# The second MLP of an RWKV and two-MLP kernel: Strassen's method for its input product, tokens as the moving operand of its output product

## The chip, the cores and the metric

The kernel is one program on one core of a Trainium2 chip. The metric is the device time of one execution in microseconds (us). The engines that matter are TensorE (PE in the rows; PEld is its weight load), VectorE (DVE), ScalarE (ACT), GpSimd (POOL) and SyncE (SP, which only starts DMA transfers here). Each engine works through its own queue of instructions in order, and they wait for one another by semaphores.

## The reference, cut to what matters

```python
# attention: batch 4, 8 heads, 768 steps, head size 48
for t in range(S):
    cur = np.einsum('bhd,bhe->bhde', u[None] * kt, vt)
    y[:, :, t] = np.einsum('bhd,bhde->bhe', rt, state + cur)
    state = wt[:, :, :, None] * state + np.einsum('bhd,bhe->bhde', kt, vt)
x = y as (3072 tokens, 384)
# first MLP: 384 -> 1536 (gated) -> 384
x = (x @ w_a) * (x @ w_b) @ w_out
# second MLP: 384 -> 2048 -> 384
h = x @ w_in
g = np.maximum(h, 0.0) + alpha * np.minimum(h, 0.0)
return g @ w_out
```

All inputs and the output are float32. The kernel gets close to float32 products by splitting every operand into a high and a low part (`hi`, `lo`) and adding three products: high by high, low weight by high, high weight by low. Each `128x128` by `128x512` product is therefore three matmuls.

## The kernel before, in words

The attention and the first MLP run interleaved and are not touched in what they compute. The first MLP ends by writing its result, tile by tile, to a scratch tensor in DRAM (`x2d`).

The second MLP (`mlp2`, L1098) then takes the 3072 tokens in six chunks `c` of 512 (128 steps of each of the four sequences) and the 2048 features in 16 groups `f` of 128. For each chunk, `load_x2` (L1067) reads 384 x 512 values back and splits them. For each group, `gh` makes `h` = three contraction tiles by three part products = nine matmuls with 512 token columns moving, into a PSUM bank (`hp`, `hb`). DVE applies the leaky function (`neg`, `pos`: L1145, L1149), ACT makes the high part of `g` (L1154) and DVE the low part (L414, the helper `tt`). The output product `out2` has `g` as the stationary operand (128 features x 128 tokens) and the weights as the moving one: 384 columns, four token tiles, three part products, twelve matmuls for each `f` and `c`, into four accumulators (`acd0` to `acd2` and `hb2`). Four groups' input products and four groups' output products alternate (`RUN = 4`), so PSUM holds four `h` banks and four accumulators. A finished chunk is copied out by ACT and DVE (L1191, L1189) and stored by SP with rows of 1536 bytes (L1194).

The weights are loaded once (`load_w`, L427, DMAs from the POOL queue at L443) and turned into high and low parts by ACT (L453, L464) and DVE (L459, L468). All 32 tiles of the second MLP stay in SBUF for all chunks.

The order of all instructions is made before the build by a planner (`Tasks`). Each piece of work is added with its engine, an estimated duration, a priority, what it reads and writes, and the buffer that it takes; a list scheduler runs forward in time, keeps what is urgent by a backward pass, repeats this eight times and issues the best order. All stages pass through it together, so a change in the second MLP also shifts the order of earlier work.

Of the kernel before, what the change touches and what calls it, by code (L numbers as in the profile page):

```python
# [367 lines left out]
def rwkv_then_moe_kernel(  # L368
# [698 lines left out]
    def load_x2(c, p):  # L1067
        st = {}
        xn = f"xx{c}"
        for kt in range(3):  # L1070
            s = f"x2r{c}_{kt}"

            def ld(kt=kt):
                st[kt] = P2["p"].tile([128, 512], F32, tag="x2r", name="x2r", bufs=3)
                for i in range(2):
                    nc.sync.dma_start(out=st[kt][:, 256 * i:256 * i + 256], in_=x2d[2 * c + i, :, kt])

            def hi(kt=kt):
                if kt == 0:
                    X["2", c] = xp.tile([128, 2, 3, 512], F32R, tag="x", name="x", bufs=2)  # L1080
                nc.scalar.copy(X["2", c][:, 0, kt], st[kt])

            def lo(kt=kt):
                tt(X["2", c][:, 1, kt], st[kt], X["2", c][:, 0, kt].bitcast(F32), ALU.subtract)

            add("SP", 1.2, p - 20, ld, r=[f"x2d{2 * c}_{kt}", f"x2d{2 * c + 1}_{kt}", "p2"], w=[s], alloc=("x2r", s), nbytes=128 * 2048, packet=1024)
            add("ACT", act(512), p, hi, r=[s], w=[f"{xn}/{kt}h"], alloc=("x", xn) if kt == 0 else None)
            add("DVE", dve(512), p, lo, r=[s, f"{xn}/{kt}h"], w=[f"{xn}/{kt}l"])
        return [f"{xn}/{kt}{z}" for kt in range(3) for z in "hl"]
# [294 lines left out]
```

## Time and profile before

| | us |
|---|---|
| runs (three) | 991.46, 991.49, 995.54 |
| median | 991.49 |
| the profiled execution: its own time | 992.03 |
| its span, first to last instruction | 990.3 |
| PE busy | 973.9 (98%) |
| DVE busy | 713.6 (72%) |
| ACT busy | 366.8 (37%) |
| POOL busy | 60.6 (6%) |

The profile shows one execution; its own time is 0.5 us above the median of the runs, and 1.7 us longer than its span. Busy shares are means over stages that differ much, so the stage of the second MLP has to be cut out by time. Matmuls overlap, so the duration in a row (390 ns for one of 512 columns) is longer than the distance from one to the next.

### The profile page before, as it was taken

What the parts mean: (1) busy time and instruction counts of PE and PEld (TensorE: products, weight loads), DVE (VectorE), ACT (ScalarE), POOL (GpSimd) and SP (SyncE); (2) the same over time, 40 slices, a digit from 0 to 9 for tenths busy, and PEclk for the clock granted to TensorE, in tenths of its full rate; (3) what the DMA queues carried; (4) which work ended last, traced back from release to release, by engine and by line L of the source; (5) the groups of instructions that cost most, each with busy time, mean ns of one, the idle gap of its engine ahead of it and who ended that gap; (6) DMA issues with size and microseconds to landing.
All of it is one profiled execution on the core that took longest, in us unless ns stands there. A gap on an engine that the chain in (4) does not pass through costs nothing.

```text
span 990.3 us, 20850 instructions
## 1 busy us (share of the span) xinstructions
PE 973.9 (98%) x8802; PEld 821.1 (83%) x8802; DVE 713.6 (72%) x1215; ACT 366.8 (37%) x783; POOL 60.6 (6%) x113
## 2 busy tenths in 40 slices
PE   7999999999999999999999999999999999999998
PEld 3668777888888887887888888999999999999998
DVE  8989999797989999989735784555463645554543
ACT  0667572625444445452536662211111212111111
POOL 1111111000100100010003211000000000000000
PEclk9999999999999999999999999999999999999999
DMA  8897963404243342433026640020100100000000
GB/s 217 192 260 215 258 155 97 131 18 131 54 127 88 109 115 61 112 102 103 15 75 198 195 152 33 1 64 1 32 33 1 32 32 1 32 1 1 33 1 32
DMA packets 84559, 86.97 MB, mean 88 GB/s; under 512 B 62001, under 2 KB 71345, under 8 KB 83185
## 3 DMA queue, kind: packets, MB, share of 16 engines
q1 hardware_dynamic: 77296, 54.18, 21.1%
q0 software_dynamic: 7168, 31.45, 10.2%
q8 instruction: 69, 1.13, 0.5%
q14 instruction: 26, 0.20, 0.1%
HBM read 73.22 MB, written 11.01 MB: 85 GB/s over the span
## 4 chain that ended last, share of the span: by engine, by line
PE 78%; DVE 12%; issue 4%; DMA 3%; ACT 1%; POOL 1%; SPq 0%; DVEq 0%; POOLq 0%; ACTq 0%
PE acd L964 15%; PE hb L964 15%; PE pb L964 11%; PE acc L964 11%; PE pa L964 11%; PE hp L964 10%; DVE Tp L414 3%; DVE e L414 2%; DVE A L631 2%; PE psl L712 2%; PE psx L878 1%; DMA Tp<-in_rkw_t_dram 1%; DMA N<-in_rkw_n_dram 1%; DVE T L414 1%; DVE N L414 1%
## 5 line engine op out<-in xcount | busy, mean ns | idle before, releaser
L964 PE MATMUL acd<-w,g 128*128 128x384 f32 x864 | 192.6, 335 | 0.0
L1154 ACT CAST g<-g 128x512 fp32r<-128x512 f32 x96 | 59.7, 622 | 306.4 <-DVE g L1149 215.8
L964 PE MATMUL acc<-g,w 128*128 128x512 f32 x648 | 172.4, 396 | 0.0
L964 PE MATMUL pb<-x,w 128*128 128x512 f32 x648 | 160.5, 392 | 1.9 <-DVE a L414 1.9
L964 PE MATMUL pa<-x,w 128*128 128x512 f32 x648 | 162.1, 395 | 0.0
L964 PEld LDWEIGHTS acd<-w,g 128*128 128x128 f32 x864 | 154.2, 188 | 1.8
L1145 DVE TENSOR_SCALAR g<-hp,al 128x512 f32<-128x512 f32 x48 | 36.0, 751 | 156.2 <-PE hp L964 156.2
L964 PEld LDWEIGHTS pb<-x,w 128*128 128x128 f32 x648 | 121.0, 188 | 28.8 <-DVE a L414 3.4
L964 PEld LDWEIGHTS pa<-x,w 128*128 128x128 f32 x648 | 121.8, 189 | 26.9 <-issue 0.5
L964 PEld LDWEIGHTS acc<-g,w 128*128 128x128 f32 x648 | 118.8, 188 | 24.6
L414 DVE TENSOR_TENSOR Tp<-Tp 112x1024 f32<-112x1024 f32 (+2 forms) x132 | 106.6, 807 | 2.6 <-DMA Tp<-in_rkw_t_dram 2.1
L964 PE MATMUL hb<-x,w 128*128 128x512 f32 x432 | 102.9, 391 | 0.0
L964 PE MATMUL hp<-x,w 128*128 128x512 f32 x432 | 102.0, 389 | 0.0
L964 PEld LDWEIGHTS hp<-x,w 128*128 128x128 f32 x432 | 81.1, 188 | 16.8
L964 PEld LDWEIGHTS hb<-x,w 128*128 128x128 f32 x432 | 80.8, 188 | 16.0
L964 PE MATMUL hb<-w,g 128*128 128x384 f32 x288 | 92.5, 335 | 0.0
L1030 ACT CAST g<-a 128x512 fp32r<-128x512 f32 x72 | 44.6, 620 | 115.6 <-DVE a L414 90.9
L631 DVE TENSOR_REDUCE A<-e 128x16 f32<-128x768 f32 (+15 forms) x148 | 85.6, 578 | 0.9
L414 DVE TENSOR_TENSOR g<-g,g 128x512 fp32r<-128x512 f32 x96 | 64.1, 685 | 22.8 <-ACT g L1154 22.3
L414 DVE TENSOR_TENSOR a<-a,pb 128x512 f32<-128x512 f32 x72 | 49.1, 681 | 35.4 <-PE pb L964 35.2
L1021 ACT COPY a<-pa 128x512 f32<-128x512 f32 x72 | 41.9, 582 | 48.6 <-PE pa L964 40.4
L414 DVE TENSOR_TENSOR g<-a,g 128x512 fp32r<-128x512 f32 x72 | 49.4, 686 | 10.9 <-ACT g L1030 10.8
(80 smaller groups left out, 972.6 us busy)
## 6 DMA issues: line engine op xcount, KB each, us to landing
raw<-in_wt_dram POOLq DMA_DIRECT2D x68, 383.8 KB, 3.9
Tp<-in_rkw_t_dram SPq DMA_DIRECT2D x33, 448.0 KB, 6.6
N<-in_rkw_n_dram SPq DMA_DIRECT2D x10, 1152.0 KB, 5.5
x2d<-x POOLq DMA_DIRECT2D x36, 128.0 KB, 2.2
x2r<-x2d SPq DMA_DIRECT2D x36, 128.0 KB, 2.2
out_dram<-o SPq DMA_DIRECT2D x24, 192.0 KB, 1.9
V<-in_v_s_dram SPq DMA_DIRECT2D x11, 384.0 KB, 3.2
Z<-in_v_s_dram SPq DMA_DIRECT2D x44, 96.0 KB, 3.0
```

The costliest lines, as they stand in the source:

```text
L414: nc.vector.tensor_tensor(out=out, in0=a, in1=b, op=op)
L631: nc.vector.tensor_reduce(out=v[:, :, d:d + (n - 1) * (SUB + 1) + 1:SUB + 1], in_=part(st["e"], 0, n), axis=AX.X, op=ALU.add)
L712: nc.tensor.matmul(out=st["ps"][o0:o0 + ms, cc, q, zc * i:zc * i + zc], lhsT=t[b0:b0 + 48, 1, q0 + q, t0:t0 + ms], rhs=r[b0:b0 + 48, q0 + ...
L878: nc.tensor.matmul(out=st["ps"][32 * g:32 * g + 32, s // 4, 64 * cc:64 * cc + 64], lhsT=zt(cc, hd)[:, 4 * b + q, c0:c0 + 32], rhs=mt(hd)[: ...
L964: nc.tensor.matmul(out=out, lhsT=lhsT, rhs=rhs, start=start, stop=stop)
L1021: nc.scalar.copy(c["as", f, half][:, cs], c["a", f, half][:, cs])
L1030: nc.scalar.copy(c["g", f][:, 0, cs], c["as", f, half][:, cs])
L1145: nc.vector.tensor_scalar(out=st["m", f], in0=st["h", f], scalar1=0.0, scalar2=al[:, f:f + 1], op0=ALU.min, op1=ALU.mult)
L1154: nc.scalar.copy(st["g", f][:, 0], st["m", f])
```

## The change

The second MLP is rewritten. It works in cells: a pair of feature groups (`e` = 0 to 7, groups 2e and 2e+1) by a pair of blocks of 512 tokens. There are three passes `p` over the tokens (1024 tokens each) with eight cells in a pass.

- **Input product.** Two of the three contraction tiles are multiplied by Strassen's method in Winograd's form: seven block products in place of eight, with sums of token blocks (`t1` to `t4`, made by POOL in `load_x2`) and of weight blocks (`ws`, `wc`, made by POOL in `load_c`). The third contraction tile stays as four products. A cell has 11 block products of three matmuls, 33, in place of 36. The sums of the products are built in PSUM: bank X is accumulated in four steps, and after each of the first three ACT copies its state to SBUF (`snap`, L1223); bank Y has one such copy. The four results are then formed by DVE (`done`: a sum with a bank), followed by two ACT instructions (Relu) and one DVE instruction for the leaky function, and ACT and DVE for the high and low part of `g`.
- **Output product.** The weights are the stationary operand and `g` the moving one, with 512 tokens: nine matmuls for each group and block, into three accumulators for each of the two blocks (`oc00` to `oc12`). The results are transposed against the output's layout: DVE transposes blocks of 32 x 32 (`leave`, L1297) and the stores have runs of 128 bytes (L1304). In the last pass half of the stores are issued from the ACT queue.
- **Weights.** Five tiles for each `e` (`wi`, `ws`, `wc`, two `wp`), 40 in all. They do not stay in SBUF: pass 0 writes them to a DRAM scratch (`keeps`, L1178), passes 1 and 2 read them back on the SP queue (`again`, L1185).
- Some attention tiles (`M`, `Z`, `St`, `A16`) move to a pool that is freed after the attention.

```diff
+    def load_x2(p, pr):
...
+        split("b11", "xr00")
+        split("b22", "xr11")
+        comb("xr10", "xr11", "xr10", ALU.subtract)
+        split("t3", "xr10")
+        comb("xr00", "xr10", "xr00", ALU.add)
+        split("t2", "xr00")
...
+    def load_c(e, pr):
...
+        for i in range(4):
+            add(*SENG, pr, lambda i=i: sums(i), r=[r0, r1], w=[r1])
...
+    def keeps(e, pr):
+        for k, nm in CELL(e, 0):
+            add("SP", 0.6, pr, lambda k=k: nc.sync.dma_start(out=wsd[WI[k]], in_=W[k].bitcast(F32).rearrange("p z n -> p (z n)")),
+                r=[nm, nm + "/l"], w=[f"kept{nm}"], nbytes=128 * 3072)
+
+    def again(e, p, pr):
+        for (k, nm), (k0, nm0) in zip(CELL(e, p), CELL(e, 0)):
+            def ld(k=k, k0=k0):
+                W[k] = wp.tile([128, 2, 384], F32R, tag="w", name="w", bufs=NW)
+                nc.sync.dma_start(out=W[k].bitcast(F32).rearrange("p z n -> p (z n)"), in_=wsd[WI[k0]])
...
+            def snap(bank, o):
+                add("ACT", 0.58, pr - 20, lambda: nc.scalar.copy(SL[tm[o]], b[bank]), r=[f"h{bank}"], w=[tm[o]])
+
+            def done(bank, o, f, n):
+                x, q, g = tm[o], f"TQ{o % NQ}", f"G{par}{o}"
+                s = SL
+                add("DVE", 0.69, pr - 20, lambda: tt(s[x], s[x], b[bank], ALU.add), r=[f"h{bank}", x], w=[x])
+                if ACTP:
+                    add("ACT", 0.62, pr - 20, lambda: nc.scalar.activation(out=s[q], in_=s[x], func=ACTF.Relu, scale=-1.0), r=[x], w=[q])
+                    add("ACT", 0.62, pr - 20, lambda: nc.scalar.activation(out=s[x], in_=s[x], func=ACTF.Relu), r=[x], w=[x])
+                    add("DVE", 0.69, pr - 20, lambda: nc.vector.scalar_tensor_tensor(
+                        out=s[x], in0=s[q], scalar=al[:, f:f + 1], in1=s[x], op0=ALU.mult, op1=ALU.subtract), r=[x, q, "al"], w=[x])
...
+            pe(X, [(lambda: WA(0), "b11")], [nA], True, False)
+            snap(X, 0)
+            pe(Y, [(lambda: WB(0), "t1")], [nB], True, False)
+            snap(Y, 3)
+            pe(X, [(lambda: WB(1), "t2")], [nB], False, False)
+            snap(X, 1)
+            pe(Y, [(lambda: WC(0), "b22"), (lambda: WA(2), "b32")], [nA, nC], False, True)
+            done(Y, 1, 2 * e, 1)
+            pe(X, [(lambda: WB(2), "t3")], [nB], False, False)
+            snap(X, 2)
+            pe(U, [(lambda: WA(1), "b21"), (lambda: WA(2), "b31")], [nA], True, True)
+            done(U, 0, 2 * e, 0)
+            pe(X, [(lambda: WC(2), "b32")], [nC], False, True)
+            done(X, 3, 2 * e + 1, 1)
+            pe(V, [(lambda: WC(1), "t4"), (lambda: WC(2), "b31")], [nC], True, True)
+            done(V, 2, 2 * e + 1, 0)
...
+                        for m in ms:
+                            mm(acc[n, m], W[kw][:, wi, 128 * m:128 * m + 128], SL[g][:, gi], f == 0 and i == 0, f == F2 - 1 and i == 2)
...
+        def leave(n, m, pr, name):
+            o = f"O{(6 * p + 3 * (1 - n) + m) % NO}"
+            add("DVE", 0.69, pr - 20, lambda: nc.vector.transpose(SL[o], acc[n, m]), r=[name], w=[o])
...
+                    eng = (nc.sync, nc.scalar)[i % 2] if p == 2 else nc.sync
+                    eng.dma_start(
+                        out=out[row:row + k, 128 * m + 32 * i:128 * m + 32 * i + 32].rearrange("(j a) b -> a j b", a=32),
+                        in_=SL[o][32 * i:32 * i + 32, at:at + k].rearrange("a (j b) -> a j b", b=32))
...
-        for f in range(F2):
-            step(f, pr(f))
-            if f % RUN == RUN - 1:
...
+        for e in range(NE):
+            cell(e, pr(e))
+            if e:
+                outs(e - 1, pr(e))
+            elif tail:
+                tail.pop()(pr(0))
```

**First place: TensorE (PE) where the first MLP hands over to the second.** Before, the input products of the second MLP stand in whole groups of nine (`hp`, `hb`), with what is left of the first MLP (`acc`) between them:

```order
L964 MATMUL acc1_6648<-g2_7206,w_1958 128x512 x3
L964 MATMUL acc2_6649<-g2_7206,w_1958 128x512 x3
L964 MATMUL hb0_6442<-x_6514,w_6753 128x512 [waits DVE_49]
L964 MATMUL hb0_6442<-x_6514,w_6753 128x512 x8
L964 MATMUL hb1_6448<-x_6514,w_6768 128x512 [waits DVE_49]
L964 MATMUL hb1_6448<-x_6514,w_6768 128x512 x8
L964 MATMUL hp_7302<-x_6514,w_6713 128x512 x9
L964 MATMUL hp_7316<-x_6514,w_6734 128x512 x9
```

Now, in the second cell of pass 0 (names `hx0_1`, `hy0_1`, `hu0_1`, `hv0_1` are the banks X, Y, U, V of pass 0, e = 1):

```order
L1198 MATMUL hx0_1_7301<-xs_6449,w_6843 128x512 [waits DVE_49]
L1198 MATMUL hx0_1_7301<-xs_6449,w_6843 128x512 x2
L1198 MATMUL hy0_1_7311<-xs_6453,w_6862 128x512 [waits DVE_49]
L1198 MATMUL hy0_1_7311<-xs_6453,w_6862 128x512 x2
L1198 MATMUL hx0_1_7301<-xs_6455,w_6862 128x512 [waits Activation_49]
L1198 MATMUL hx0_1_7301<-xs_6455,w_6862 128x512 x2
L1198 MATMUL hy0_1_7311<-xs_6450,w_6865 128x512 [waits Activation_49]
L1198 MATMUL hy0_1_7311<-xs_6450,w_6865 128x512 x2
L1198 MATMUL hy0_1_7311<-xs_6456,w_6843 128x512 x3
L1198 MATMUL hx0_1_7301<-xs_6457,w_6862 128x512 [waits Activation_49]
L1198 MATMUL hx0_1_7301<-xs_6457,w_6862 128x512 x2
L1198 MATMUL hu0_1_7348<-xs_6452,w_6843 128x512 [waits DVE_49]
```

Steps of three and six matmuls on two banks now follow one another, and each waits for ACT or DVE to have read the bank of the step before last; in this one cell no other matmuls stand between them.

**Second place: TensorE in a later cell** (pass 1, e = 5; `oc` are output products of the cell before):

```order
L1198 MATMUL hx1_5_8799<-xs_7713,w_8544 128x512
L966 MATMUL oc10_8337<-gx_6543,w_8469 128x512
L966 MATMUL oc11_8351<-gx_6543,w_8469 128x512
L966 MATMUL oc12_8374<-gx_6543,w_8469 128x512
L1198 MATMUL hu1_5_8838<-xs_6453,w_8517 128x512 [waits DVE_49]
L1198 MATMUL hu1_5_8838<-xs_6453,w_8517 128x512 x2
L1198 MATMUL hu1_5_8838<-xs_6455,w_8517 128x512 x3
L1198 MATMUL hx1_5_8799<-xs_6449,w_8554 128x512 [waits Activation_49]
L1198 MATMUL hx1_5_8799<-xs_6449,w_8554 128x512 x2
L966 MATMUL oc00_8399<-gx_6543,w_8469 128x512
L966 MATMUL oc01_8420<-gx_6543,w_8469 128x512
L966 MATMUL oc02_8428<-gx_6543,w_8469 128x512
```

The order of the whole cell is X 3, Y 3, output 6, X 3, Y 6, X 3, output 3, U 6, X 3, output 6, V 6, output 21 matmuls: output products stand between most of the steps.

**Third place: the DMA queue of SP at the end.** Before, its last stores are four of 128 rows, each waiting for its copy:

```order
L1194 DMA out_0_dram<-o_9622 128x384 [waits DMAHW6_49,DVE_49]
L1194 DMA out_0_dram<-o_9993 128x384 [waits DMAHW7_49,Activation_49]
L1194 DMA out_0_dram<-o_9998 128x384 [waits DMAHW0_49,DVE_49]
L1194 DMA out_0_dram<-o_10004 128x384 [waits DMAHW1_49,Activation_49]
L1194 DMA out_0_dram<-o_10007 128x384 [waits DMAHW2_49,DVE_49]
```

Now there are 24 on this queue and as many on that of ACT, for the six results of the last pass:

```order
L1304 DMA out_0_dram<-tm_7850 32x8x32 [waits DMAHW0_49,DVE_49]
L1304 DMA out_0_dram<-tm_7850 32x8x32 [waits DMAHW2_49]
L1304 DMA out_0_dram<-tm_7850 32x8x32 [waits DMAHW4_49]
L1304 DMA out_0_dram<-tm_7850 32x8x32 [waits DMAHW6_49]
L1304 DMA out_0_dram<-tm_7882 32x8x32 [waits DMAHW0_49,DVE_49]
L1304 DMA out_0_dram<-tm_7882 32x8x32 [waits DMAHW2_49]
L1304 DMA out_0_dram<-tm_7882 32x8x32 [waits DMAHW4_49]
L1304 DMA out_0_dram<-tm_7882 32x8x32 [waits DMAHW6_49]
```

Each store covers 32 partitions with 256 runs of 128 bytes, and each waits for the fourth store before it on the same queue, since four semaphores (`DMAHW0`, `2`, `4`, `6`) serve it.

## Rows read from the trace of the kernel before

**Rows 1.** The page: busy time by engine, and granted clock in 40 slices.

```profile
PE 973.9 (98%) x8802; PEld 821.1 (83%) x8802; DVE 713.6 (72%) x1215; ACT 366.8 (37%) x783; POOL 60.6 (6%) x113
...
PEclk9999999999999999999999999999999999999999
```

**Rows 2.** Busy time in three stretches (us): PE, PEld, DVE, ACT, POOL; clock; DMA.

```profile
100.00:480.00 380.00, 375.63 (x4851) 307.09 (x4852) 353.31 (x619) 179.21 (x402) 19.78 (x37) 1.00 0.41 108
480.00:584.00 104.00, 104.00 (x610) 85.96 (x609) 60.19 (x117) 59.15 (x116) 19.88 (x37) 1.00 0.48 142
584.00:986.00 402.00, 402.00 (x2040) 366.47 (x2039) 207.98 (x322) 77.56 (x132) 3.21 (x6) 1.00 0.06 21
```

**Rows 3.** Groups by line: the second MLP's matmuls; count, then busy us, mean ns.

```profile
L964 PE MATMUL acd<-w,g 128*128 128x384 f32 x864 | 192.6, 335 | 0.0
...
L964 PE MATMUL hb<-x,w 128*128 128x512 f32 x432 | 102.9, 391 | 0.0
L964 PE MATMUL hp<-x,w 128*128 128x512 f32 x432 | 102.0, 389 | 0.0
L964 PE MATMUL hb<-w,g 128*128 128x384 f32 x288 | 92.5, 335 | 0.0
```

**Rows 4.** Timeline of PE at the hand-over: start us, length, instruction.

```profile
575.05 2.20 PE L964 MATMUL pb<-x,w 128*128 128x512 f32 x9
577.09 1.52 PE L964 MATMUL acc<-g,w 128*128 128x512 f32 x6
...
584.57 2.20 PE L964 MATMUL hp<-x,w 128*128 128x512 f32 x9
```

**Rows 5.** Timeline, output products of the last chunk.

```profile
974.38 0.33 PE L964 MATMUL hb<-w,g 128*128 128x384 f32 x1
...
975.07 0.33 PE L964 MATMUL hb<-w,g 128*128 128x384 f32 x1
```

**Rows 6.** Timeline, the end of the kernel.

```profile
984.26 1.72 PE L964 MATMUL acd<-w,g 128*128 128x384 f32 x9
984.98 0.48 ACT L1191 COPY o<-acd 128x384 f32<-128x384 f32 x1 [8.18 <-PE acd L964]
985.48 1.98 SPq L1194 DMA_DIRECT2D out_dram<-o  x4
...
985.82 0.69 PE L964 MATMUL hb<-w,g 128*128 128x384 f32 x3
```

**Rows 7.** Groups by line: the nearest ACT and DVE instructions to the new ones.

```profile
L1154 ACT CAST g<-g 128x512 fp32r<-128x512 f32 x96 | 59.7, 622 | 306.4 <-DVE g L1149 215.8 <-PE hb L964 84.2 <-DVE g L414 5.8
...
L414 DVE TENSOR_TENSOR a<-a,pb 128x512 f32<-128x512 f32 x72 | 49.1, 681 | 35.4 <-PE pb L964 35.2
...
L453 ACT ACTIVATE ws<-raw 128x384 f16<-128x384 bf16 x68 | 42.3, 640 | 24.4 <-DMA raw<-in_wt_dram 14.5 <-DVE raw L459 6.7 <-issue 1.3
L1021 ACT COPY a<-pa 128x512 f32<-128x512 f32 x72 | 41.9, 582 | 48.6 <-PE pa L964 40.4 <-DVE g L414 7.9
...
L464 ACT ACTIVATE w<-raw 128x384 fp32r<-128x384 f32 x68 | 36.9, 546 | 15.1 <-PE pa L964 11.1 <-DVE raw L459 2.3 <-DVE w L468 1.2
```

**Rows 8.** Timeline, from a DVE instruction to the ACT instruction that waits for it.

```profile
703.87 0.69 DVE L1149 SCALAR_TENSOR_TENSOR g<-hp,g 128x512 f32<-128x512 f32 x1
704.67 0.62 ACT L1154 CAST g<-g 128x512 fp32r<-128x512 f32 x1 [9.17 <-DVE g L1149]
```

**Rows 9.** Timeline of SP: eight transfers of 256 runs each.

```profile
234.11 5.28 SPq L663 DMA_DIRECT2D M<-mb  x8
```

**Rows 10.** The page: DMA issues, KB each, median us from issue to landing.

```profile
out_dram<-o SPq DMA_DIRECT2D x24, 192.0 KB, 1.9
...
M<-mb SPq DMA_DIRECT2D x88, 16.0 KB, 2.3
...
Z<-St SPq DMA_DIRECT2D x8, 72.0 KB, 7.3
```

**Rows 11.** Busy time in one stretch with four Z transfers alone (columns as in rows 2).

```profile
202.00:208.00 6.00, 6.00 (x98) 5.07 (x87) 6.00 (x10) 3.10 (x6) 0.00 (x0) 1.00 0.37 68
```

**Rows 12.** Groups by line: GpSimd's own work before.

```profile
L1209 POOL MEMSET Z<- 128x2048 f32 x1 | 1.8, 1805 | 0.3 <-POOLq L1371 0.3
```

More of the change, by code (lines that the diff above doesn't have):

```diff
@@ L1065, in mlp1 @@
             add("Pool", 2.08, pr(F1) - 50, st, r=[x2], w=[f"x2d{u}_{m}" for u in us], nbytes=128 * 4 * n, packet=1024)
[L1067 to L1089, printed above, removed]
@@ new lines, in CELL, with take @@
+    def CELL(e, p):
+        c = ((("i", 2 * e), f"wi{2 * e}"), (("ws", e), f"ws{e}"), (("wc", e), f"wc{e}"), (("p", 2 * e), f"wp{2 * e}"),
+             (("p", 2 * e + 1), f"wp{2 * e + 1}"))
+        return c if p == 0 else [(k + (p,), f"{n}p{p}") for k, n in c]
+    WI = {k: i for i, k in enumerate(k for e in range(8) for k, _ in CELL(e, 0))}
+    GX = {"GA": ["G00", "G01", "G02"], "GB": ["G03", "G10", "G11"]}
+    def take(tag, names, make, parts=("",)):
+        for n in names:
+            add("HOST", 0, 0, lambda n=n: make(n), r=["p2"], w=[n + z for z in parts], alloc=(tag, n) if tag else None)
@@ new lines, in make_r, with make_o, make_g, make_g2 @@
+        def make_r(n):
+            SL[n] = P2["p"].tile([128, 512], F32, tag="x2r", name="x2r", bufs=6)
+        def make_o(n):
+            SL[n] = P2["p"].tile([128, 512], F32, tag="o", name="o", bufs=1)
+        def make_g(n):
+            t = xp.tile([128, 2, 3, 512], F32R, tag="x", name="gx", bufs=2)
+            for i, g in enumerate(GX[n]):
+                SL[g] = t[:, :, i]
+        def make_g2(n):
+            SL[n[1:]] = xp.tile([128, 2, 512], F32R, tag="g2", name="gs", bufs=2)
+        take(None, [f"X{i}" for i in range(9)], make_x, ("/h", "/l"))
@@ new lines, in rwkv_then_moe_kernel, with finish @@
+        held2 = None
+        def finish(x, i):
+            if x:
+                g, hs, e, q = x
+                for _ in (g, *hs)[i]:
+                    pass
+                if i == 2:
+                    keeps(e, q)
+        for e in range(8):
+            q = start[NB - 1] + 4 + 9 * e
+            g = load_c(e, q)
+            hs = [load_w(("p", 2 * e + i), wt2[2 * e + i, 1], q + 3, ["p2"]) for i in range(2)]
+            next(g)
+            finish(held2, 0)
+            next(g)
+            finish(held2, 1)
+            next(hs[0])
+            finish(held2, 2)
+            next(hs[1])
+            held2 = g, hs, e, q
+            if e == 0:
+                take("w", tms[:-2], make2)
@@ new lines, in rwkv_then_moe_kernel @@
+        for i in range(3):
+            finish(held2, i)
+        take("w", [f"X{i}{z}" for i in range(9, 14) for z in "hl"], make_xh)
+        take("w", [f"O{i}" for i in range(1, NO)], make2)
+        for p in range(3):
+            load_x2(p, start[NB - 1] if p == 0 else s2 + d * p - 30)
+            if p:
+                for e in range(8):
+                    again(e, p, s2 + d * p + d / 8 * e - 20)
+            mlp2(p, lambda e, s=s2 + d * p: s + d / 8 * e)
+        tail.pop()(s2 + 3 * d)
```

275 lines of the change are left out of this document (168 added, 107 removed).

## The prediction

> **What bounds the kernel now.** I read the page's busy times first [rows 1]: TensorE is busy in 98% of the span, at the full granted clock (2.4 GHz) in every slice. That is a mean, so I cut the span at the start of the second MLP. There [rows 2] (the last of the three) PE is busy in 402.00 of 402.00 us, while DVE works 208 and ACT 78. So nothing that only relieves DVE or ACT can help; time goes only if matmuls go or get closer together. The durations in the groups (335 and 390 ns, [rows 3]) overlap and can't be summed, so I take distances of starts. At the hand-over nine matmuls of 512 columns take 577.09 - 575.05 = 2.04 us [rows 4], 0.2267 us each. Among output products, four of 384 columns lie between 974.38 and 975.07 [rows 5], 0.1735 us each. The sum checks: 864 input products x 0.2267 = 195.9, 1152 output products (864 + 288, [rows 3]) x 0.1735 = 199.9, and the order leaves 21 matmuls of the first MLP behind the second's first one, 4.8: together 400.5. The trace has from 584.57 [rows 4] to the end of the last matmul's place, 985.82 + 3 x 0.1735 = 986.34 [rows 6], 401.8. So 1.3 us is lost in the whole stage: there are no stalls to win, and every stall that the change brings is paid in full.
>
> **What it removes.** Per cell 33 matmuls for the input product in place of 36, and 24 cells: 792 in place of 864, 72 fewer, 16.3 us. The output product has 16 groups x 6 blocks x 9 = 864 matmuls of 512 columns in place of 1152 of 384: 195.9 against 199.9, 4.0 us. With the same 21 of the first MLP, PE's floor is (792 + 864 + 21) x 0.2267 = 380.2 us. Against the 401.8 that the stage took: **-21.6 us**.
>
> One rule of the skill speaks against the second part: the Trainium skill, "TensorE: Matmul & The Clock Gate", section "Back-to-back issue gap", gives an isolated warm gap of N/2.4 + 2.5 ns, so 215.8 ns for 512 columns and 162.5 for 384. By it the output product would gain nothing (186.5 against 187.2 us) and the input product 15.5. The rows show about 11 ns more per matmul at either width, and I go by them.
>
> **What the other engines now do.** The nearest rows for the new instructions [rows 7]: a `snap` is the copy of a bank by ACT, 0.582; a Relu or the high part on ACT, 0.622; a sum with a bank on DVE, 0.681, and the other DVE steps I take as that. A cell gives ACT 4 x 0.582 + 12 x 0.622 = 9.8 us and DVE 12 x 0.68 = 8.2, beside PE's 69 x 0.2267 = 15.6. Neither is the bound by sum; what counts is whether PE finds a bank read in time. Latencies: the third matmul of 984.26 has its place until 984.78, and ACT starts on its bank at 984.98 [rows 6], 0.20; from DVE's end at 704.56 to ACT's start at 704.67 is 0.11 [rows 8], and I take the same for ACT or DVE to PE.
>
> Walk through a later cell (second pair of order rows), us from its start: X 0.00 to 0.68, Y to 1.36, output to 2.72, X to 3.40, Y to 4.76, X to 5.44, output to 6.12, U to 7.48, X to 8.16, output to 9.52, V to 10.88, output to 15.64. The second X needs the first copy: 0.68 + 0.20 + 0.58 + 0.11 = 1.57, wanted at 2.72. In the same way Y is ready at 2.25 for 3.40, the third X at 4.29 for 4.76, U (after a DVE sum) at 5.75 for 6.12, the fourth X at 6.33 for 7.48, V at 8.47 for 9.52. All hold, with 0.37 us or more to spare, as long as ACT and DVE take up the item at once. One other item ahead of it (0.62 or 0.68) makes the third X 0.15 late and U 0.31, so a cell loses 0 to 0.5 us; 22 cells, 0 to 11. I take 1, near the lower end, since ACT and DVE idle over a third of a cell.
>
> The second cell of pass 0 (first pair of order rows) has no output products between its steps. The same walk there gives waits of 0.21 before the second X, 0.31 before U, 0.31 before V and 0.31 before the next cell's Y: 1.1 us; with one weight conversion ahead of each (about 0.55 on ACT, [rows 7]) up to 3.5. I take 2. At the two changes of pass six DVE transposes of some 0.7 come between; their cover is a cell's output matmuls, and I give 0 to 2, take 1. Stalls together: **+4 us** (1 to 14).
>
> The weights of passes 1 and 2 come back through SP's queue, 5 tiles in a 15.6 us cell; they are asked for some two cells ahead, and DMA is busy for 0.06 of the time there now [rows 2]. I cost them at nothing; the 24 stores of the pass before stand in the same queue, at 0.66 us apiece (below) 16 us, which two cells' lead (31 us) covers.
>
> GpSimd's sums are new: 12 of 512 columns and 32 of 128, against only fills and DMA descriptors before. The one wide row is a fill of 2048 columns in 1.8 us [rows 12], 0.45 for 512 columns at its rate, the lower bound for a sum; four times that, 1.8, is my upper one. Both are hidden: at most 12 x 1.8 + 32 x 0.5 = 38 us over a pass and more.
>
> The first MLP's order shifts too. Between 100 and 584 us PE idles 4.4 us [rows 2], so there is little to win; I take 0, within -2 to +3.
>
> **The end.** Now the kernel ends 990.3 - 986.34 = 4.0 us after PE. From the last DMA's issue to the end is 4.0 - 0.20 - 0.56 (the copy's length) = 3.2, of which landing is 1.9 [rows 10]. With the change each of SP and ACT issues 24 stores of 256 runs. The first accumulator is complete 33 matmuls before the last, -7.5 us; with 0.20, a transpose of 0.7 and 0.11 the first store can start at -6.5. Eight transfers of 256 runs took SP 5.28 us [rows 9], 0.66 each. The 24th starts at -6.5 + 23 x 0.66 = 8.7, lands 2.3 later (M, [rows 10]) and the end is 1.3 behind: 12.3 after PE, **+8.3 us**. Lower bound: 1.98 / 4 = 0.50 for a store now [rows 6], which gives 8.2 and +4.2. Upper bound: each store waits for the fourth before it, so six landings in series; the slowest landing of short runs is 7.3 (Z<-St, [rows 10]), which gives -6.5 + 43.8 + 1.3 = 38.6 and +34.6. I go by the M row because its run count is the same. The 16 engines are no bound if writes cost what reads do: four Z transfers, 2048 runs of 192 bytes, kept them busy 0.37 x 6.0 us [rows 11], 17.3 ns a run and engine; 12,288 runs are 13.3 us, less than the 15.8 of issue.
>
> **The sum.** The profiled execution took 992.0: 992.0 - 21.6 + 4 + 8.3 = 982.7. The median of the runs is 0.5 lower, so I forecast **982.2 us**, 0.9% faster; the likeliest case by itself spans 976 to 989.
>
> **Rivals.**
> - *The stores of the last pass land slowly.* For it: runs of 128 bytes, four in flight per queue, and the 7.3 us row. Against it: M and the out stores land in 2.3 and 1.9. It decides from 4.5 us of landing on: then the end grows by 17.6 and the whole gain is gone. At 7.3 the time is 982.2 + 34.6 - 8.3 = 1008.5, slower. The Trainium skill ("DMA: Bandwidth & Descriptors", Specifications) states that below 512 bytes a transfer is a read-modify-write; no row here has a short write to DRAM.
> - *ACT or DVE answers late in every cell.* For it: 0.37 us of slack, and in pass 0 the weight conversions go on: from the first copy of its second cell to that of its fourth, ACT has 58 instructions, 35.2 us by [rows 7], PE 144 matmuls, 32.6. Against it: after that ACT has 9.8 of 15.6 us. At 0.5 us a cell it is 982.2 + 10 = 992, no change.
> - *The output product gives nothing.* If a matmul's place went by columns alone, 512 columns would take 0.1735 x 4/3 = 0.2313 there and 864 of them 199.9 us, as much as now; 4.0 us less gain is 986.2, at the border of no change. Against it: [rows 4] are of the same form (weights stationary, 512 tokens moving) and have 0.2267.
> - The change could fail to remove the 72 matmuls; the order shows them gone, so I give it nothing.
>
> **How the numbers follow.** Forecast 0.55; slow landing 0.15; late answers 0.17; no gain from the output product 0.08; anything else, the first MLP's order or weights that come late, 0.05. A measurement of this kernel can tell 0.5% from no change: below 986.5 is faster, above 996.5 slower. Faster: 0.52 of the forecast and 0.03 of the third, 0.55. Slower: 0.10 of slow landing, 0.05 of late answers, 0.03 of the rest, 0.18. The same: 0.27. The range runs from 975 (end +4, stalls 1, 2 won in the first MLP, rounded down) to 1000, where half of the slow landings are left out.
>
> **What the next profile would show.** Matmuls `h` 792 and `oc` 864, at 0.227 us between starts; from the first `hx` to the last matmul 380 us and a few; a dent in PE's digits only near the start of pass 0; ACT at some 60% and DVE at 50% of the stage; after the last matmul 12 us of stores, 0.66 apart on two queues. I am wrong if PE idles more than 0.5 us in a later cell, if the stores are over 1 us apart, or if the second MLP starts later than 587.

## The result, and the profile after

The changed kernel takes **979.35 us** (median of four runs, 978.45 to 979.88) against 991.95 us of the kernel before in runs on the same chip: ratio 0.986, 95% interval 0.984 to 0.989. The forecast was 982.2. The profiled execution took 978.45 us, the fastest of the four, and its span is 976.6; that of the kernel before was 990.3, so 13.7 us went.

The page of the changed kernel, busy times and granted clock [rows 1]:

```profile
PE 953.7 (98%) x8442; PEld 768.8 (79%) x8442; DVE 739.2 (76%) x1238; ACT 528.5 (54%) x1076; POOL 97.2 (10%) x157
...
PEclk9999999999999999999999999999999999999999
```

TensorE is as full as before and has 360 matmuls fewer (8802 to 8442): 72 of the input product, 288 of the output product. The same in three stretches, cut at the second MLP's first matmul and at the end of the last one's place (columns as in [rows 2]):

```profile
100.00:480.00 380.00, 374.48 (x4841) 305.43 (x4841) 352.11 (x619) 175.25 (x397) 19.32 (x36) 1.00 0.40 107
480.00:586.00 106.00, 104.96 (x611) 86.15 (x610) 59.71 (x105) 55.49 (x109) 35.14 (x54) 1.00 0.59 197
586.27:968.35 382.08, 381.39 (x1678) 314.26 (x1676) 232.82 (x354) 244.86 (x433) 24.25 (x33) 1.00 0.43 129
```

The last row is the stage: 382.1 us for 401.8, with DVE busy for 61% of it and ACT for 64%. The timeline of TensorE has its two ends [rows 4, 6]:

```profile
586.27 0.84 PE L1198 MATMUL hx<-xs,w 128*128 128x512 f32 x3
...
966.31 2.20 PE L966 MATMUL oc<-gs,w 128*128 128x512 f32 x9
```

From 586.27 to 966.31 + 9 x 0.2267 = 968.35. The floor worked out ahead was 380.2, so 1.9 us are stalls. All of them lie in the second cell of pass 0, the one without output products between its steps:

```profile
598.55 0.86 PE L1198 MATMUL hx<-xs,w 128*128 128x512 f32 x3
599.63 0.96 PE L1198 MATMUL hy<-xs,w 128*128 128x512 f32 x3 [0.22 <-DVE tm L414]
600.42 0.86 PE L1198 MATMUL hx<-xs,w 128*128 128x512 f32 x3
601.50 1.67 PE L1198 MATMUL hy<-xs,w 128*128 128x512 f32 x6 [0.22 <-ACT tm L1223]
603.00 0.84 PE L1198 MATMUL hx<-xs,w 128*128 128x512 f32 x3
604.01 1.67 PE L1198 MATMUL hu<-xs,w 128*128 128x512 f32 x6 [0.17 <-DVE tm L414]
...
607.96 0.84 PE L966 MATMUL oc<-gx,w 128*128 128x512 f32 x3
```

From 598.55 to 607.96 stand 33 matmuls, 7.48 us at 0.2267, and they take 9.41. The brackets name who was late: the copies and sums that free a bank. By the starts, Y waits twice for 0.40 us, U for 0.33 and V for 0.26, 1.4 in all; the steps right behind these waits then take 0.11 to 0.15 us more than their places, 0.5 in all. Later the distance from one cell's V step to the next's is 15.64 us, 69 places of 0.2267, or, where the order differs, another whole number of places.

The end, transposes and stores [rows 6, 9]:

```profile
963.86 10.62 SPq L1304 DMA_DIRECT2D out_dram<-tm  x20
963.86 10.39 ACTq L1304 DMA_DIRECT2D out_dram<-tm  x20
...
967.19 2.08 DVE L1297 STREAM_TRANSPOSE tm<-oc 128x512 f32<-128x512 f32 x3 [2.00 <-PE oc L966]
```

976.6 - 968.35 = 8.25 us lie behind TensorE, for 3.96 before. A store takes its queue 0.52 to 0.53 us here on average (10.62 / 20), the transposes are done at 969.27, and the queues issue until 974.5. The average holds waits: some stores waited for the fourth before them to land, on SP (us in total, times, longest)

```profile
SPq L1304 <- DMA out_dram<-tm: 0.7, 2, 0.4
```

Experiment 7 below ends with the same stores, and there SP's queue waits for no landing; a store takes 9.97 / 20 = 0.50:

```profile
967.97 9.97 SPq L1304 DMA_DIRECT2D out_dram<-tm  x20
```

The page gives the landing of these stores as 1.7 us on SP and 1.9 on ACT [rows 10].

The span's difference is the sum of three: the second MLP starts at 586.27 for 584.57, +1.7; the stage -19.7; the end +4.3; together -13.7.

### The profile page after: what moved, and what is told of

Its sections match the earlier page's. It is cut to its first block, busy times and chain, and to the rows that moved or that the text cites. A ratio compares the mean times of both kernels' runs of the same rounds, so it can differ in the third digit from the quotient of the medians.

```text
span 976.6 us, 20832 instructions
## 1 busy us (share of the span) xinstructions
PE 953.7 (98%) x8442; PEld 768.8 (79%) x8442; DVE 739.2 (76%) x1238; ACT 528.5 (54%) x1076; POOL 97.2 (10%) x157
## 4 chain that ended last, share of the span: by engine, by line
PE 68%; DVE 21%; DMA 5%; issue 3%; ACT 1%; POOL 1%; SPq 0%; ACTq 0%; DVEq 0%; POOLq 0%
PE oc L966 19%; PE acc L966 8%; PE pb L966 8%; PE pa L966 8%; PE hx L1198 6%; PE hy L1198 5%; DVE Tp L414 4%; DVE e L414 4%; DVE A L633 3%; PE hu L1198 3%; PE hv L1198 3%; PE warm L1335 2%; PE psl L714 2%; DVE N L414 2%; DMA raw<-in_wt_dram 2%
## 5 line engine op out<-in xcount | busy, mean ns | idle before, releaser
L966 PE MATMUL oc<-gx,w 128*128 128x512 f32 x648 | 162.8, 389 | 0.0
L966 PEld LDWEIGHTS oc<-gx,w 128*128 128x128 f32 x648 | 121.6, 188 | 25.3
L1223 ACT COPY tm<-hx 128x512 f32<-128x512 f32 x72 | 42.3, 588 | 77.9 <-PE hx L1198 77.3
L1198 PE MATMUL hx<-xs,w 128*128 128x512 f32 x288 | 80.9, 389 | 0.0
L1232 DVE SCALAR_TENSOR_TENSOR tm<-tm,al 128x512 f32<-128x512 f32 x96 | 72.7, 760 | 5.2 <-ACT tm L1231 5.1
L1230 ACT ACTIVATE tm<-tm 128x512 f32<-128x512 f32 x96 | 60.1, 627 | 24.5 <-DVE tm L414 24.0
L414 DVE TENSOR_TENSOR tm<-tm,hy 128x512 f32<-128x512 f32 x24 | 16.5, 688 | 73.1 <-PE hy L1198 73.1
L1198 PEld LDWEIGHTS hx<-xs,w 128*128 128x128 f32 x288 | 54.1, 188 | 11.3
L1231 ACT ACTIVATE tm<-tm 128x512 f32<-128x512 f32 x96 | 59.9, 625 | 1.4
L453 ACT ACTIVATE ws<-raw 128x384 f16<-128x384 bf16 x68 | 42.8, 642 | 31.3 <-DVE raw L459 15.3
```

The lines of the kernel that those rows point to most:

```text
L414: nc.vector.tensor_tensor(out=out, in0=a, in1=b, op=op)
L453: nc.scalar.activation(out=c["s"].bitcast(F16).rearrange("p (n b) -> p n b", b=2)[:, :, 1], in_=c["raw"].bitcast(BF16)[:, :, 2], func=ACTF ...
L966: nc.tensor.matmul(out=out, lhsT=lhsT, rhs=rhs, start=start, stop=stop)
L1198: nc.tensor.matmul(out=ps, lhsT=wt[:, wi, at:at + 128], rhs=SL[xs[k][xi]], start=first and n == 0, stop=last and n == 2, skip_group_check= ...
L1223: add("ACT", 0.58, pr - 20, lambda: nc.scalar.copy(SL[tm[o]], b[bank]), r=[f"h{bank}"], w=[tm[o]])
L1230: add("ACT", 0.62, pr - 20, lambda: nc.scalar.activation(out=s[q], in_=s[x], func=ACTF.Relu, scale=-1.0), r=[x], w=[q])
```

## The experiments

Each kernel ran beside the kernel before on one chip; the ratio is to that one. "Stage" is from the second MLP's first matmul to the end of the last one's place, "end" what follows in the span, both from the profile.

**1. Input product plain, the rest as changed.**

```diff
-            pe(X, [(lambda: WA(0), "b11")], [nA], True, False)
-            snap(X, 0)
...
+            for bank, w, nm, ks, o, mi, n in (
+                    (X, WA, nA, ("t1", "b22", "b32"), 1, 0, 1), (Y, WA, nA, ("b11", "b21", "b31"), 0, 0, 0),
+                    (U, WB, nB, ("t1", "b22", "b32"), 3, 1, 1), (V, WB, nB, ("b11", "b21", "b31"), 2, 1, 0)):
+                pe(bank, [(lambda w=w, k=k: w(k), x) for k, x in enumerate(ks)], [nm], True, True)
```

> The changed kernel with the input product computed plainly: per cell four banks of nine matmuls in place of the 33 of Strassen's method, the four bank copies by ACT gone, the DVE sum with a bank replaced by a DVE copy of it, no sums on GpSimd. Output product, blocks, reload of weights and stores as in the changed kernel. Theory (the gain is the number of matmuls): 864 h matmuls for 792, 72 x 0.2267 = 16.3 us more, less the 2 us of stall that the second cell has now: 979.4 + 16.3 - 2 = 993.7, between 993 and 996, no faster than the kernel before. Rival (Strassen's chain of copies and sums costs as much as it saves, and the gain comes from the output product): 980 to 985.

990.98 us, ratio 0.999 (0.997 to 1.001): no faster than the kernel before. Timeline:

```profile
583.66 2.20 PE L1166 MATMUL hx<-xs,w 128*128 128x512 f32 x9
...
978.06 2.20 PE L966 MATMUL oc<-gs,w 128*128 128x512 f32 x9
```

The stage is 980.10 - 583.66 = 396.4 us, 14.4 more than in the changed kernel: 16.3 for 72 matmuls, less the 1.9 of stalls, which are gone. The time is below the 993 to 996 expected; in the profiled execution the second MLP starts at 583.66, 2.6 us earlier than in the changed kernel's, and that is about the difference. The rival falls.

**2. Output product alone, in the kernel before.**

```diff
...
-                    mm(st["acc"][t], st["g", f][:, gi, 128 * t:128 * t + 128], W["p", f][:, wi],
+                    mm(st["acc"][t], W["p", f][:, wi, 128 * t:128 * t + 128], st["g", f][:, gi],
...
```

> The kernel before with only the output product turned round: three accumulators of 128 features x 512 tokens, 864 matmuls of 512 columns for 1152 of 384, DVE transposes, and stores of 128-byte runs (per pass 48 stores of 128 runs, on two queues in the last pass); input product plain. Theory (a matmul's place is 0.2267 us at 512 columns and 0.1735 at 384): from the first hp to the end of the last matmul's place 401.8 - 4.0 = 397.8 us. Rival (the place goes by columns alone): 401.8. The end grows whichever holds: first accumulator ready 6 matmuls before the last, 24 stores per queue at 0.25 to 0.5 us each, landing 2.1 and 1.3 behind it: 9 to 15 us after PE for 4.0, so 992 - 4 + 5 to 11 = 993 to 999 in all, slower than the kernel before, by the first theory.

996.87 us, ratio 1.004 (1.003 to 1.006), slower. Timeline:

```profile
584.09 2.20 PE L964 MATMUL hp<-x,w 128*128 128x512 f32 x9
...
964.38 16.48 PE L964 MATMUL acd<-g,w 128*128 128x512 f32 x72
...
980.28 11.30 SPq L1193 DMA_DIRECT2D out_dram<-o  x24
```

The stage is 964.38 + 72 x 0.2267 - 584.09 = 396.6 us, 5.2 less than 401.8: the 4.0 of the matmuls' places, and most of the 1.3 by which the kernel before was longer than the sum of its places. (Those 1.3 were no waits: no two starts there lie more than 0.012 us further apart than a place.) The rival by columns falls. The end is 994.5 - 980.7 = 13.8 us, which takes more than that back. A store of 128 runs takes 0.47 us (11.30 / 24).

**3. Long runs in the last stores.**

```diff
-                        out=out[row:row + k, 128 * m + 32 * i:128 * m + 32 * i + 32].rearrange("(j a) b -> a j b", a=32),
+                        out=out[row:row + k, 128 * m + 32 * i:128 * m + 32 * i + 32].rearrange("(j a) b -> a j b", a=32) if p < 2 else out[row:row + k].rearrange("r c -> (r c)").rearrange("(q a j b) -> q a j b", q=12, a=32, b=32)[4 * m + i],
```

> The changed kernel, but the 48 stores of the last pass write rows of 1 KB (32 rows a store, 32 KB in one piece of DRAM) in place of 256 runs of 128 bytes; the last pass's results so stand in the wrong places of the output. Theory (the end is bound by the issue of the stores, 0.47 us each for 256 runs, 24 on a queue): short issues end with the last accumulator, 0.2 + 0.72 + 0.1 + a few stores + landing of some 2 + 1.3, so 4.5 to 6 us after PE for 8.25 and 975.5 to 977. Rival (the bytes or the landing bind the end): 8 us after PE and 979.4.

978.48 us, ratio 0.986 (0.983 to 0.988), as the changed kernel. Timeline:

```profile
965.47 9.68 SPq L1304 DMA_DIRECT2D out_dram<-tm  x20
...
967.93 2.20 PE L966 MATMUL oc<-gs,w 128*128 128x512 f32 x9
```

The end is 977.7 - 969.97 = 7.7 us, not the 4.5 to 6 of the theory, and a store still takes 0.48. Six executions with the short runs (the changed kernel, experiments 1, 5, 6, 7 and 8) end 7.9 to 8.6 us behind TensorE, so the long runs win little if anything. Issue binds, as the theory had it, but it hardly goes by the runs: 32 rows of 1 KB cost the queue nearly what 256 runs of 128 bytes cost. The number of stores counts, as experiment 10 confirms.

**4. A third queue.**

```diff
-                    eng = (nc.sync, nc.scalar)[i % 2] if p == 2 else nc.sync
+                    eng = {"S": nc.sync, "A": nc.scalar, "P": nc.gpsimd}[("SAPS", "APSA", "PSAP" if n else "SASA")[m][i]] if p == 2 else nc.sync
```

> The changed kernel, with the last pass's 48 stores on three queues: SP 18, ACT 18, GpSimd 12; order otherwise the same. Theory (issue binds): 18 x 0.47 = 8.5 us in place of 11.3, but not less than the last accumulator's eight stores allow: 0.2 + 0.72 + 0.1 + 4 x 0.47 + 2.1 + 1.3 = 6.3 us after PE for 8.25: 977.4. Rival (the 16 DMA engines bind, busy 0.63 to 0.70 of the time there): 8 us after PE, 979.4. If GpSimd takes over 1 us to issue a store, its 12 end later than the others and the gain is lost.

979.76 us, ratio 0.986 (0.984 to 0.988): nothing won. The last matmul's place ends at 970.86, the span at 979.9, so the end is 9.0 us. SP's row:

```profile
966.36 10.28 SPq L1304 DMA_DIRECT2D out_dram<-tm  x14
```

A store took SP 0.73 us now, though it had fewer of them; the median landing on SP rose from 1.7 to 2.2, and on GpSimd's queue it was 2.9. SP's waits in this stretch:

```profile
SPq L1304 <- DVE tm L1297: 2.3, 2, 1.8
SPq L1304 <- DMA out_dram<-tm: 1.3, 3, 0.7
```

So SP ran out of stores and waited for a transpose, until 970.42; from then on the three queues issued together, their stores landed more slowly, and each had to wait for the fourth before it. With three queues the landing binds, not the issue, which speaks for the rival.

**5. Every bank copy twice.**

```diff
-                add("ACT", 0.58, pr - 20, lambda: nc.scalar.copy(SL[tm[o]], b[bank]), r=[f"h{bank}"], w=[tm[o]])
+                add("ACT", 0.58, pr - 20, lambda: [nc.scalar.copy(SL[tm[o]], b[bank]) for _ in range(2)], r=[f"h{bank}"], w=[tm[o]])
```

> The changed kernel with each of the 96 bank copies by ACT (4 a cell, 24 cells) done twice, 0.58 us more each; order of every engine otherwise the same. Theory (a later cell has slack behind its copies: 1.15 us before the second X, 1.15 before Y, 0.47 before the third X, 1.15 before the fourth): only the third X is late, by 0.58 - 0.47 = 0.1 us a cell, and by up to 0.6 where another ACT item stands in front: 22 cells give 2 to 13, I take 4; the second cell of pass 0 loses 2 more: stage 382.1 + 2 to 15, time 982 to 994. Rival (ACT's queue is never what PE waits for, it is 62% busy): stage 382 to 383, time 979 to 980. Rival (PE waits at every copy): 96 x 0.58 = 56 us.

988.53 us, ratio 0.995 (0.993 to 0.997); stage 978.40 + 2.04 - 589.30 = 391.1, 9.1 more. A usual cell takes 15.87 us for 15.64, which makes 2.8 in twelve cells; six cells, five of them around the changes of pass, lose 0.6 to 0.9 each, and 1.8 falls on the start of pass 0. The Y, third X and next step of one cell, in the changed kernel and then here:

```profile
791.55 1.52 PE L1198 MATMUL hy<-xs,w 128*128 128x512 f32 x6
792.91 0.84 PE L1198 MATMUL hx<-xs,w 128*128 128x512 f32 x3
793.59 0.84 PE L966 MATMUL oc<-gx,w 128*128 128x512 f32 x3
```

```profile
784.23 1.52 PE L1198 MATMUL hy<-xs,w 128*128 128x512 f32 x6
785.69 0.96 PE L1198 MATMUL hx<-xs,w 128*128 128x512 f32 x3
786.49 0.85 PE L966 MATMUL oc<-gx,w 128*128 128x512 f32 x3
```

Y's six places are over at 785.59 and the third X starts at 785.69: 0.10 late for a copy 0.58 longer, so the slack is 0.48 us; the walk ahead of the result gave 0.47. The three matmuls behind the wait take 0.80 in place of 0.68, so the cell loses 0.22. That is the margin on which the change lives.

**6 and 7. Twice as many reloads.** First each load was done twice into the same tile, then a copy to DRAM scratch was put behind each.

```diff
-                nc.sync.dma_start(out=W[k].bitcast(F32).rearrange("p z n -> p (z n)"), in_=wsd[WI[k0]])
+                for _ in range(2):
+                    nc.sync.dma_start(out=W[k].bitcast(F32).rearrange("p z n -> p (z n)"), in_=wsd[WI[k0]])
```

> The changed kernel with each of the 80 loads that bring the weights back in passes 1 and 2 done twice, one behind the other, each 384 KB. Theory (asked for two cells ahead, the reload is hidden with room to spare: 5 loads of some 3 us landing in a cell of 15.6): stage and time the same, 382 and 979.4, within 1 us. Rival (the loads or their queue are near their limit): weights late in passes 1 and 2, PE idle behind a DMA there, 5 x 3.1 - or more a cell, up to 16 x 1 to 3 us.

1059.3 us, ratio 1.066 (1.063 to 1.069); stage 461.7. Neither theory was tested: the second load of a tile waits for the first to land, and with it all that is queued behind. Waits of SP's queue (total, times, longest):

```profile
SPq L1186 <- DMA w<-wsd: 265.6, 80, 4.7
```

```diff
...
-                nc.sync.dma_start(out=W[k].bitcast(F32).rearrange("p z n -> p (z n)"), in_=wsd[WI[k0]])
+                nc.sync.dma_start(out=W[k].bitcast(F32).rearrange("p z n -> p (z n)"), in_=wsd[WI[k0]]); nc.sync.dma_start(out=wsx[40 * p - 40 + WI[k0]], in_=wsd[WI[k0]])
```

> The changed kernel with one more DMA behind each of the 80 loads that bring the weights back, on the same queue and from the same place, but to DRAM scratch that nothing waits for; so the queue and the DMA engines carry twice as many transfers of 384 KB, and no transfer waits for the one before it (in the run that did each load twice the second waited for the first to land, 265.6 us of waits on SP). Theory (the reload is hidden with room to spare): stage 382 and time 979.4, within 1.5 us. Rival (the reload is near a limit): PE idle in passes 1 and 2, stage over 390.

981.06 us, ratio 0.988 (0.985 to 0.990). The stage is 970.43 + 2.04 - 590.38 = 382.1, the same to a tenth; only the start is later. Pass 1 in the changed kernel and then here (columns as in [rows 2]):

```profile
712.00:837.00 125.00, 125.00 (x553) 103.52 (x552) 73.31 (x110) 77.77 (x136) 1.76 (x2) 1.00 0.48 134
```

```profile
712.00:837.00 125.00, 125.00 (x553) 103.49 (x552) 74.22 (x111) 78.76 (x137) 2.59 (x2) 1.00 0.82 275
```

TensorE stays full with the DMA engines at 0.82 and twice the bytes. The transfers are hidden with room to spare; a load that must wait for another on the same queue is not.

**8. Without GpSimd's sums.**

```diff
-            add(*XENG, pr, lambda: (nc.gpsimd if XENG[0] == "Pool" else nc.vector).tensor_tensor(out=SL[out_], in0=SL[a], in1=SL[b], op=op), r=[a, b], w=[out_])
+            add(*XENG, pr, lambda: nc.gpsimd.tensor_tensor(out=SL[out_][:, 0:4], in0=SL[a][:, 0:4], in1=SL[b][:, 0:4], op=op), r=[a, b], w=[out_])
...
-            (nc.gpsimd if SENG[0] == "Pool" else nc.vector).tensor_tensor(out=o, in0=a, in1=b, op=op)
+            nc.gpsimd.tensor_tensor(out=v(r1, 0, 0)[:, 0:4], in0=v(r1, 0, 1)[:, 0:4], in1=v(r0, 0, 0)[:, 0:4], op=op)
...
```

> The changed kernel with GpSimd's sums cut to 4 columns (12 that had 512 columns, 32 that had 128); the Strassen weights and token sums are so not formed, and the two weights of a pair are copies of the first plane. Order on PE, DVE, ACT and SP the same. Theory (GpSimd's sums cost what they hold up DVE: where one ran, a DVE instruction beside it took up to 1.79 us for 0.69): the second MLP starts up to 1 to 3 us earlier, 584 to 585.5 after the start, and the second cell of pass 0 loses less than 2 us: 975.5 to 978. Rival (the later start is the new order of the first MLP and what else differs between executions, and GpSimd's work is hidden): start 586 to 589, 979 to 980.

979.98 us, ratio 0.986 (0.982 to 0.989): no difference to be seen in the time, and the start was at 587.82. But executions differ in the first 100 us, before any of this: TensorE is busy there for 92.42 us in the changed kernel's profile and 90.18 in this one. So compare the stretch before the second MLP, and the group of DVE instructions on line 414 that form `xs` in it; the changed kernel, then this one:

```profile
480.00:580.00 100.00, 98.96 (x585) 81.16 (x584) 56.02 (x98) 51.97 (x102) 31.18 (x47) 1.00 0.57 187
```

```profile
L414 DVE TENSOR_TENSOR xs<-x2r,xs 128x512 fp32r<-128x512 f32 x9 | 8.8, 1008 | 0.3 <-ACT xs L1114 0.3
```

```profile
480.00:580.00 100.00, 99.84 (x648) 82.31 (x641) 52.95 (x102) 51.62 (x102) 19.76 (x47) 1.00 0.57 182
```

```profile
L414 DVE TENSOR_TENSOR xs<-x2r,xs 128x512 fp32r<-128x512 f32 x9 | 5.8, 686 | 0.3 <-ACT xs L1114 0.3
```

GpSimd's sums slow the DVE instruction from 686 to 1008 ns on average and cost TensorE 0.9 us (1.04 idle for 0.16). This is no accident of one execution: experiments 3 to 7 run this order with the sums, and each idles 1.0 to 1.2 us there. The stage is 382.1 in both, so the second cell's 1.9 us are not theirs. Half of the theory holds.

**9. Passes in another order.**

```diff
-    BLOCKS2 = [[(t, 0, 4)] for t in range(4)] + [[(t, 4, 2), (t + 1, 4, 2)] for t in (0, 2)]
+    BLOCKS2 = [[(t, 0, 4)] for t in (0, 1)] + [[(t, 4, 2), (t + 1, 4, 2)] for t in (0, 2)] + [[(t, 0, 4)] for t in (2, 3)]
```

> The changed kernel with the passes in another order: the two blocks made of two runs of 256 tokens go to the second pass, so that the last pass stores 24 times 512 runs of 128 bytes in place of 48 times 256. Theory from the two runs on stores (a store holds its queue 0.47 us whether it has 32, 128, 256 or 512 runs): 12 stores a queue, 5.6 us, no longer bind; the end goes by the last accumulator: 0.92 to the end of its transpose, 0.1, two stores 0.94, landing 3.3, 1.3 behind it: 6.6 us after PE for 8.25, time 977.7. Rival (the issue goes by the runs, 0.94 us for 512): 8.2 us after PE, 979.4. Stage 382 in both.

975.87 us, ratio 0.983 (0.980 to 0.986), the fastest kernel here that writes every result to its place, though its interval overlaps that of the changed kernel. Stage 382.0; the end is 976.9 - 969.39 = 7.5 us, 0.75 less where 1.65 was expected.

```profile
965.95 7.33 ACTq L1304 DMA_DIRECT2D out_dram<-tm  x10
...
967.35 2.20 PE L966 MATMUL oc<-gs,w 128*128 128x512 f32 x9
```

A store takes 0.73 us here, and again that is waiting: on SP's queue 1.6 us for the landing of earlier stores and 1.0 for transposes; the median landing on ACT's queue is 3.0. The next run shows why.

**10. The same with long runs.** The edit is that of 3.

> The kernel with the passes in another order, with the last pass's 24 stores writing rows of 2 KB in place of 512 runs of 128 bytes (results in the wrong places of the output). There the 24 stores took 0.70 to 0.73 us each with the DMA engines' share at 1.2 to 1.4, for 0.47 expected. Theory (with fewer stores the 12,288 runs of 128 bytes, by the DMA engines' time for each, bind the end): with long rows 0.47 us a store, and the end 0.92 + 0.1 + 0.94 + 1.7 + 1.3 = 5.0 us after PE for 7.5; time 973.4. Rival (the stores' bytes or the landing as such): 7.5 us after PE, 975.9.

975.04 us, ratio 0.982 (0.979 to 0.984).

```profile
965.61 5.92 ACTq L1304 DMA_DIRECT2D out_dram<-tm  x10
...
967.10 2.20 PE L966 MATMUL oc<-gs,w 128*128 128x512 f32 x9
```

The end is 974.3 - 969.14 = 5.2 us. The median landing on ACT's queue fell to 2.1 us. With 24 stores the many short runs bind, through the landing; with 48 (experiment 3) it was the number of stores. The changed kernel's end stands near both limits.

**11 and 12. Sums on DVE**, in the kernel of 9: the weight sums alone, then all.

```diff
-    XENG, SENG = ("Pool", 1.3), ("Pool", 0.45)
+    XENG, SENG = ("Pool", 1.3), ("DVE", 0.2)
```

In 12 the first pair is `("DVE", 0.69)` too.

> The kernel with the passes in another order, and the 32 sums of weights (128 columns) moved from GpSimd to DVE, planned at 0.2 us each. Theory (GpSimd's sums cost about 0.9 us of PE between 480 and 580 by holding up DVE, as the run without sums showed, and 32 sums of 0.2 us on DVE cost less): 0 to 1 us less than with them on GpSimd, 975 to 976; the order of the first MLP shifts, which can move it by 1 or 2 us either way. Rival (DVE is fuller before the second MLP, and the sums delay it): 977 to 979.

> As the kernel before it, with the 12 sums of token blocks (512 columns) on DVE too, planned at 0.69 us: GpSimd then adds nothing. Theory: PE idle between 480 and 580 as in the kernel before the change (0 to 0.2 us) and 975 to 976; 8.3 us more on DVE in three passes where it is half busy cost nothing. Rival (in the first cells of pass 0 DVE is what PE waits for): the second cell loses 1 to 3 us more, 976 to 979.

977.19 us, ratio 0.985 (0.982 to 0.987), and 977.14, 0.984 (0.982 to 0.986). TensorE is busy for 100.00 of the 100 us from 480 in both, for 99.41 in 9 and 10, so the 0.6 us that GpSimd cost there is gone; the stages are 382.0 and 382.1. The times don't tell the three kernels apart.

## Why the prediction was right, point by point

- **The bound.** Right: the time went with the matmuls. Experiment 1 gives the input product 14.4 us net, experiment 2 the output product 5.2. By itself the turned output product makes the kernel no faster (experiments 1 and 2), since its stores take 4 to 10 us at the end; what the change wins beyond that is the 72 matmuls. Strassen's method with the old output product was not tried. ACT came out at 64% of the stage for some 60 forecast, DVE at 61 for 50, which cost nothing outside the second cell.
- **-21.6 us on TensorE.** Right to 0.1: the floor of 380.2 and 1.9 of stalls make 382.1. The places of 0.2267 and 0.1735 us held, and the output product gained its 4.0 (experiment 2). By the isolated gap in the Trainium skill, "TensorE: Matmul & The Clock Gate", section "Back-to-back issue gap", it would have gained next to nothing; the measurement decides against that.
- **Stalls, +4.** Measured 1.9. The second cell was forecast at 2 and cost 1.9; the 1 for later cells and the 1 for changes of pass cost nothing. That the 2 came out so well is in part luck: the walk had 1.1 in four waits and the rest was an allowance for weight conversions. U and V waited as it said (0.33 and 0.26 for 0.31), the second X did not, Y waited twice instead, and 0.5 is what the steps behind a wait lose, which the walk did not have. The rival of late answers in every cell falls with that; experiment 5 shows that it was near, 0.48 us of slack away.
- **Reload at nothing, GpSimd's sums at nothing.** The first right by experiment 7. The second nearly: 0.9 us of TensorE, in the first MLP, not in the stage. A sum of 512 columns took 1.28 to 1.74 us, 1.44 on average, inside the bounds.
- **First MLP, +0 (-2 to +3).** Measured +1.7 in the profile. Between 100 and 580 TensorE idled 6.6 us for 4.4 before. 0.9 of the difference is GpSimd's. The cause of the rest is open: between 100 and 480 the changed kernel idles 5.5 us and the kernel before 4.4, but experiments 3 to 7, which run the same order, idle 3.8 to 5.2 there. In the first 100 us executions of one order differ by over 2 us too. So +1.7 belongs to one execution: in the profiles of experiments 3 to 8 the second MLP starts at 587.8 to 590.4, beyond the 587 that the prediction gave as a sign of being wrong, and its term for the first MLP is the least certain of the sum.
- **The end, +8.3.** Mis-sized: +4.3. The step that failed is "I go by the M row because its run count is the same", with 0.66 us a store; 0.48 to 0.53 was measured. The fault is not in the run count but in the average: the row's eight transfers hold waits. Its first six alone, and SP's waits in the row:

```profile
234.11 2.78 SPq L663 DMA_DIRECT2D M<-mb  x6
SPq L663 <- DMA Tp<-in_rkw_t_dram: 1.9, 2, 1.3
```

The six take 2.78 / 6 = 0.46 us each, and no two of them start more than 0.49 apart; with these the prediction's own sum gives 7.7 to 8.4 behind TensorE, +3.7 to +4.4. The spacing makes 3.0 of the 4.0 us; the landing, 1.7 for 2.3, and what lies behind it, 1.0 for 1.3, make the rest. The lower bound, from the four stores of the kernel before (0.50), came out near by luck, since each of those waited for its copy. The run count matters little: 32, 128 and 256 runs took 0.48, 0.47 and 0.50 to 0.53.
- **Slow landing.** Fell: 1.7 and 1.9 us for 4.5 needed. Short runs do cost something, 2.3 us of end when they bind (experiments 9 and 10); where the number of stores binds (experiment 3) they cost little. The Trainium skill, "DMA: Bandwidth & Descriptors", Specifications, has transfers below 512 bytes do a read-modify-write. Experiments 9 and 10 agree with a price on short runs, but do not tell a read-modify-write from the mere number of runs.
- **The range.** Its lower end does not follow from its terms: 992.0 - 21.6 + 4 + 1 - 2, less 0.5 for the median, is 972.9 and not 975. The time lies inside either way.

The sum mended: 982.7 - 4.0 (end) - 2.1 (stalls) + 1.7 (start) = 978.3, against 978.45 profiled. The forecast is as near as it is partly because the start's error stands against the other two.

## What to carry to other kernels

When TensorE is full, count matmuls and measure a matmul's place by distances of starts; such a sum, with the stalls added, held here to 0.1 us in 382. A chain through other engines costs nothing until it is late, so walk it and write down the slack, then spend the slack in an experiment to see that it is there. Price a store by single transfers that wait for nothing, not by the mean of a merged row, and count both its issues and its runs, for either can bind the end.

## What the runs showed of the hardware that was not expected

**GpSimd and DVE shut each other out when DVE's instruction has both inputs in SBUF.** In the changed kernel's timeline:

```profile
704.93 1.62 POOL L1123 TENSOR_TENSOR x2r<-x2r 128x512 f32<-128x512 f32 x1 [5.53 <-DVE xs L414]
...
705.32 1.79 DVE L1232 SCALAR_TENSOR_TENSOR tm<-tm,al 128x512 f32<-128x512 f32 x1
```

GpSimd's sum begins beside a DVE instruction and takes 1.62 us; alone such a sum takes 1.28 to 1.30. The group of line 1232 has a mean of 0.76 us; this one takes 1.79 and lasts until 707.11, 0.56 behind the end of GpSimd's sum at 706.55. The trace has eight DVE instructions of 512 columns and two SBUF inputs that began during a sum of GpSimd, and each ends 0.55 us behind that sum. A DVE sum that reads a PSUM bank is not held, nor does it hold GpSimd:

```profile
661.68 1.29 POOL L1123 TENSOR_TENSOR x2r<-x2r 128x512 f32<-128x512 f32 x1 [4.24 <-DMA x2r<-x2d]
662.55 0.69 DVE L414 TENSOR_TENSOR tm<-tm,hv 128x512 f32<-128x512 f32 x1 [1.02 <-PE hv L1198]
```

Nine of these stood beside GpSimd's sums and took 0.67 to 0.69 us, as they do alone. The Trainium skill, "SBUF — State Buffer", section "SBUF: two separate sides", describes the port pair that GpSimd and VectorE share as an exclusive lock, also for a VectorE instruction with two inputs in SBUF beside a GpSimd one that reads SBUF. The trace and experiment 8 agree.

**A store's issue is nearly the same whatever it moves**: 0.47 us for 128 runs (16 KB, experiment 2), 0.48 for 32 rows of 1 KB (experiment 3), 0.50 for 256 runs of 128 bytes where none waits for a landing (experiment 7); the last two are 32 KB.

**A wait costs TensorE more than its length**: behind the first stall of the second cell the next three matmuls took 0.79 us (599.63 to 600.42), behind that of experiment 5 0.80, in place of 0.68. The loss is in the first of the three, whose weights load only as it starts, at 599.63; in a full stream they load during the matmul before.
